# A recurrent attention layer with a soft mixture of experts: Gram quadrants, triangular blocks, transposed scans and outputs share banks, and the order is laid down anew

## The chip, the cores and the metric

One core of a Trainium2 chip runs the whole program. The time is device microseconds of one execution; several runs are taken and the median is given.

## The reference, cut to what matters

Inputs have batch 4, 8 heads, 768 positions and a head width of 40. The attention is a recurrence over positions, with a 40x40 state per batch and head:

```python
for t in range(S):
    y[:, :, t] = einsum('bhd,bhde->bhe', rt, state)
    Sa = einsum('bhde,bhe->bhd', state, at)
    state = state * wt[:, :, None, :] - einsum('bhd,bhe->bhde', Sa, bt)
    state = state + einsum('bhd,bhe->bhde', vt, kt)
```

Its output, 3072 rows of 320, goes through a soft mixture of experts: logits against 32 slots; a softmax over rows that gathers rows into slots; two matrix products (320 to 1024, a rectifier, 1024 to 320) for each of 8 experts; and a softmax over slots that spreads the result back. All of it is float32.

## The kernel before, in words

The 768 positions are cut into 12 stages of 64. The eight heads are taken in three groups `u` of 3, 3 and 2 heads (120, 120 and 80 partitions), for each of the 4 batches. In a stage:

- `scan_s`, `scan_k`, `scan_c` make running products of the decay `w` on DVE and multiply `k`, `b` and `a` by them ("wide products" of 120x768, on POOL or DVE).
- `lgram` makes the 32x32 triangular blocks of the products of `a` with `b`, and `gram` the other products of `a` with `k` and `b`: a part of 96 rows per batch (`qls`), and a quadrant of 32 rows per batch (`q0s`). Each result is cut by a mask as DVE takes it out of its PSUM bank.
- every second stage, `solve_in`, `solve_step` (30 of them, each a product and a sum, on DVE or POOL) and `solve_out` invert the triangular blocks. The very first solve is done in halves (`solve_half`, 14 steps), and `solve_join` puts the halves together by 256 small matmuls of 32x32x16: 64 in bank `jy` and, behind a copy, 64 in bank `jz`, and this for the first and the second stage of the pair.
- `chain_g`, `chain_u` (twice) and `chain_s` carry the state from stage to stage.
- `ctok_of` and `kbtok` transpose what the scans made; `y_vut`, `y_sd`, `y_p` and `y_y` make the stage's output, which goes into `xs` with the running product as a factor; the `slots_` functions feed the mixture of experts with every two stages.

Behind the last stage come the experts' products and 24 products that write the output.

All of this is recorded first as a list of operations with their dependences; eight PSUM banks are handed out as they come free. `forward` then lays the operations down, engine by engine, by a priority: the longest way to the end by its own table of costs, plus a shift per operation out of the string `SHIFT`. The string `SIDE` says for each operation that can run on two engines which of them takes it. The program's order on every engine is fixed by this. Where the planner expects TensorE to stand idle it puts in matmuls on constants (line 620, `filler`), whose results nobody reads. `HAM` and `FETCH` are its numbers for TensorE's clock and for the loading of instructions, `PACE` limits the bytes of loads in flight. Nearly every instruction carries line 1385 in the profile, that of the call that plans and emits; so the operands tell which is which: `wt` are the large work buffers, `ps` the banks, `cs_t` the constants, `mid` the buffer that holds the join's operands.

## Time and profile before

| | |
|---|---|
| median of 3 runs | 393.93 us |
| the three runs | 393.93, 388.39, 394.5 us |
| the profiled execution | 390.42 us |
| its span, first to last instruction | 388.3 us |
| TensorE: busy, share of the span | 347.5 us, 89% |
| VectorE (DVE): busy, share | 309.0 us, 80% |
| GpSimd (POOL): busy, share | 179.1 us, 46% |
| ScalarE (ACT): busy, share | 148.3 us, 38% |
| mean granted TensorE clock | 0.970 of full speed |

The profiled execution is 2.1 us longer than its span, for what lies before the first and behind the last instruction. PE is TensorE, PEld its loading of weights, SP the engine that issues the transfers. A busy PE is not PE at its peak, since matmuls overlap each other.

### The profile page before, as it was taken

The numbers are of one execution on the slowest core, as the hardware profiler recorded it, in microseconds if no ns is written. First come the engines' busy times: TensorE is split into PE (matmuls) and PEld (weight loads), VectorE is DVE, ScalarE is ACT, GpSimd is POOL, SyncE is SP. The second block draws the span as 40 slices with busy tenths as digits, with TensorE's granted clock in tenths as the row PEclk, the third lists the DMA queues.
The fourth block names the chain that finished last, engine by engine and source line by source line (L and its number), as shares of the span: only waits on it lengthen the run. The fifth ranks groups of instructions, "written<-read, shape, count | busy, mean of one in ns | idle before, by whom it ended". The sixth has DMA issues, their size and how long they took to land.

```text
span 388.3 us, 18515 instructions
## 1 busy us (share of the span) xinstructions
PE 347.5 (89%) x8179; PEld 301.5 (78%) x8179; DVE 309.0 (80%) x681; ACT 148.3 (38%) x311; POOL 179.1 (46%) x245
## 2 busy tenths in 40 slices
...
GB/s 280 382 205 285 2 45 45 126 100 71 89 163 125 68 147 112 165 102 41 137 137 122 184 111 117 104 254 183 184 128 213 282 202 197 255 329 149 2 101 307
DMA packets 37798, 60.66 MB, mean 156 GB/s; under 512 B 4695, under 2 KB 26967, under 8 KB 37719
## 3 DMA queue, kind: packets, MB, share of 16 engines
...
q8 instruction: 64, 1.05, 1.1%
...
## 4 chain that ended last, share of the span: by engine, by line
PE 57%; DVE 18%; issue 8%; DMA 7%; POOL 5%; ACT 3%; SPq 1%; DVEq 0%; POOLq 0%; ACTq 0%
PE ps L1385 56%; DVE wt L1385 11%; DMA wt<-in_kb_dram 5%; POOL wt L1385 4%; ACT wt L1385 2%; DVE mem L1385 2%; DVE ps L1385 2%; DMA wt<-in_aa_dram 1%; DVE old L1385 1%; SPq L1385 1%; DVE mid L1385 1%; PE ps L620 1%; POOL old L1385 1%; DMA wt<-in_rr_dram 0%; ACT mem L1385 0%
## 5 line engine op out<-in xcount | busy, mean ns | idle before, releaser
L1385 PE MATMUL ps<-wt,wt 128*64 128x40 f32 (+11 forms) x3576 | 163.8, 238 | 11.5 <-issue 7.2
L1385 PEld LDWEIGHTS ps<-wt,wt 80*32 80x32 f32 (+9 forms) x3576 | 142.8, 129 | 24.4 <-issue 11.2
L1385 POOL TENSOR_TENSOR old<-wt 128x130 f32<-128x130 f32 (+13 forms) x104 | 63.3, 608 | 61.1 <-DVE wt L1385 43.0
L1385 PE MATMUL ps<-cs_t,wt 120*128 120x120 f32 (+5 forms) x496 | 64.5, 267 | 12.2 <-ACT wt L1385 11.6
L1385 DVE TENSOR_TENSOR wt<-ps,cs_t 128x384 f32<-128x384 f32 (+6 forms) x132 | 61.6, 495 | 8.2 <-PE ps L1385 7.5
L1385 POOL TENSOR_TENSOR wt<-wt,wt 120x768 f32<-120x768 f32 x31 | 54.1, 1762 | 22.2 <-DVE wt L1385 14.4
L1385 POOL TENSOR_TENSOR wt<-wt,old 128x30 f32<-128x30 f32 (+13 forms) x92 | 51.6, 561 | 25.8 <-DVE old L1385 17.3
L1385 PEld LDWEIGHTS ps<-cs_t,wt 120*128 120x128 f32 (+5 forms) x496 | 50.5, 137 | 16.7 <-ACT wt L1385 12.2
L1385 ACT COPY wt<-ps 128x320 f32<-128x320 f32 (+3 forms) x62 | 30.0, 493 | 76.0 <-PE ps L1385 68.4
L1385 DVE TENSOR_TENSOR_SCAN wt<-wt,wt 120x780 f32<-120x780 f32 x24 | 44.1, 1838 | 1.7 <-DMA wt<-in_ww_dram 1.6
L1385 ACT COPY mem<-ps 120x480 f32<-120x480 f32 (+7 forms) x64 | 25.3, 412 | 35.5 <-PE ps L1385 31.6
L1385 ACT ACTIVATE wt<-ps 32x320 f32<-32x320 f32 x63 | 27.0, 429 | 30.4 <-PE ps L1385 19.0
L1385 PE MATMUL ps<-wt,mem 128*32 128x160 f32 (+4 forms) x448 | 36.9, 300 | 0.0
L1385 ACT ACTIVATE wt<-wt,bm_t 120x768 f32<-120x768 f32 (+1 forms) x36 | 28.6, 856 | 11.8 <-PE ps L1385 6.6
L1385 PE MATMUL ps<-mem 32*32 32x40 f32 (+2 forms) x776 | 32.4, 225 | 0.5 <-DVE wt L1385 0.4
L1385 PEld LDWEIGHTS ps<-wt,mem 128*32 128x32 f32 (+4 forms) x448 | 31.0, 137 | 1.7 <-issue 0.8
L1385 DVE COPY wt<-ps 128x320 f32<-128x320 f32 (+3 forms) x40 | 21.0, 544 | 7.0 <-PE ps L1385 6.7
L1385 ACT COPY wt<-wt 120x768 f32<-120x768 f32 (+3 forms) x19 | 16.2, 856 | 26.8 <-DVE wt L1385 26.7
L1385 DVE STREAM_TRANSPOSE wt<-wt 128x1024 f32<-128x1024 f32 x12 | 25.0, 2126 | 0.3
L1385 POOL MEMSET mem<- 128x2048 f32 x1 | 1.8, 1807 | 50.3 <-DVE mem L1385 50.3
L1385 DVE TENSOR_TENSOR wt<-wt,old 128x108 f32<-128x108 f32 (+16 forms) x65 | 23.3, 358 | 2.0 <-POOL old L1385 0.6
L1385 PEld LDWEIGHTS ps<-mem 32*32 32x32 f32 (+2 forms) x776 | 18.8, 116 | 7.5 <-issue 4.1
...
## 6 DMA issues: line engine op xcount, KB each, us to landing
...
```

Source lines behind the costliest of these rows:

```text
L620: self.nc.tensor.matmul(bank, lhs, rhs, start=True, stop=True)
L1385: nc.vector.memset(one_f, 0.0)
```

## The change

It makes these edits, beside new tables `SHIFT` and `SIDE` and some new numbers in the planner's model:

- `gram`: the quadrants of the three groups no longer stand beside each group's other products in its bank. They are made together, once the third group comes up, in a bank of their own, and one DVE instruction of 128x256 takes them out in place of three of 128x96, 128x96 and 128x64.
- `lgram`: the 24 products of a stage are recorded in one go at the third group rather than group by group.
- `ctok_of`: the first two groups share a bank and one copy of 128x480, in place of two of 128x240.
- `y_y`: likewise, the outputs of the first two groups share a bank, and one DVE product of 128x480 takes them out.
- `y_p`: the four products of a group, into two banks, are recorded as one operation.
- the planner's estimate of instruction loading, of TensorE's clock and of the loads in flight is changed, and the order comes out anew on each engine.

The program issues the same matmuls in the same shapes as before, 4,347 of them that compute, and 66 on constants where there were 65. Of DVE instructions there are 674 rather than 683, of ACT 298 rather than 313, of POOL 226 rather than 250; the transfers are the same in number and size. The solves' steps and sums stand 152 times on DVE (132 before) and 176 times on POOL (196 before), the wide products 10 times on DVE (6) and 28 times on POOL (32).

```diff
--- before.py
+++ after.py
@@ -126,50 +126,49 @@
 TURN = dict(PE=-70, DVE=32, ACT=18, POOL=0)
 
 
-FETCH = (256, 146, 447, 1150, 2350, 0.45)
+FETCH = (256, 146, 447, 1300, 2350, 0.5, 500)
 FILL = (900, 500, 225)
-HAM = (3413, 0.135, 1.8, 110, 0.165)
+HAM = (3413, 0.145, 1.8, 110, 0.18)
 HEAT = (0.15, 60e3, 470, 385, 400)
 DMA = (720, 1350, 1500, 1.05)
 
 CLASH = dict(DVE=138, POOL=190)
 
 ISSUE = 420
-PACE = (500e3, 60e3, 256e3, 1400e3)
+PACE = (500e3, 60e3, 256e3, 1000e3)
 WIDE, SLIM = 0.632, 1.15
 WAIT = 1500
 START = ((225, 210), (195, 195))
 ROUNDS = 0
 STEP = {**{chr(79 + v): v for v in range(-44, 46)}, "~": 13, "!": -45}
 SHIFT = (
...
 )
 SIDE = (
...
 )
 LOOK = dict(PE=1, DVE=130, ACT=1, POOL=130, SP=1)
 
@@ -632,7 +631,7 @@
                 x += m * step
                 if (self.seen - FETCH[1]) % FETCH[0] == 0:
                     r = max(x, self.there[-1] if self.there else 0.0)
-                    self.there.append(r + FETCH[3] + FETCH[5] * max(0.0, dma - r) + FETCH[4])
+                    self.there.append(r + FETCH[3] + FETCH[5] * max(0.0, dma - r - FETCH[6]) + FETCH[4])
                 if (self.seen - FETCH[2]) % FETCH[0] == 0:
                     i = (self.seen - FETCH[2]) // FETCH[0]
                     if 0 <= i < len(self.there) and self.there[i] > x:
@@ -969,15 +968,22 @@
             nc.copy_a.copy(kbks[st].rearrange("p (b c) -> p b c", b=B)[:, :, H0[u] * D:H0[u] * D + n],
                            tp[:, 0:4 * n].rearrange("p (b c) -> p b c", b=B))
 
+        ctl = {}
+
         def ctok_of(st, u):
             if u == 0:
                 ctoks.put(st)
             n = NHU[u] * D
-            tp = bank(f"tp_cs{st}")
+            if u != 1:
+                ctl[st] = bank(f"tp_cs{st}")
+            tp = ctl[st]
+            m, a = (2 * 3 * D, 3 * D * u) if u < 2 else (n, 0)
             for i in range(2):
                 o = (B * u + 2 * i) * C
-                nc.tensor.transpose(tp[:, i * n:(i + 1) * n], cps[st][0:n, o:o + 128], ident[0:n, 0:n])
-            nc.copy_a.copy(ctoks[st][:, :, H0[u] * D:H0[u] * D + n], tp[:, 0:2 * n].rearrange("p (i c) -> p i c", i=2))
+                nc.tensor.transpose(tp[:, i * m + a:i * m + a + n], cps[st][0:n, o:o + 128], ident[0:n, 0:n])
+            if u:
+                c = slice(0, m) if u == 1 else slice(H0[u] * D, H0[u] * D + n)
+                nc.copy_a.copy(ctoks[st][:, :, c], tp[:, 0:2 * m].rearrange("p (i c) -> p i c", i=2))
 
         def gram(st, u):
             if u == 0:
@@ -993,30 +999,34 @@
                 o = slice(b * w, (b + 1) * w)
 
                 nc.tensor.matmul(gr[0:96, o], k_t.rearrange("p q k t -> p (q k t)")[:, 0:96], bd[0:n, 0:nh, b, 32:64], start=True, stop=True)
-            for b in range(B):
-
-                nc.tensor.matmul(gr[32 * b:32 * b + 32, 4 * w:5 * w], kbt(st)[0:n, B * u + b, 0, 0], bd[0:n, 0:nh, b, 0:32], start=True, stop=True)
             nc.vector.tensor_tensor(
                 qls[st][0:96, 12 * u:12 * u + 4 * nh], gr[0:96, 0:4 * w].rearrange("p (h t) -> p h t", t=32),
                 mask_q[0:96].unsqueeze(1).broadcast_to([96, 4 * nh, 32]), ALU.mult)
-            nc.vector.tensor_tensor(
-                q0s[st][:, H0[u]:H0[u] + nh], gr[:, 4 * w:5 * w].rearrange("p (h t) -> p h t", t=32),
-                mask_s.unsqueeze(1).broadcast_to([128, nh, 32]), ALU.mult)
+            if u == NU - 1:
+                gq = bank(f"gq{st}")
+                for v in range(NU):
+                    n, o = NHU[v] * D, 32 * H0[v]
+                    for b in range(B):
+                        nc.tensor.matmul(gq[32 * b:32 * b + 32, o:o + 32 * NHU[v]], kbt(st)[0:n, B * v + b, 0, 0],
+                                         bds["a", st][0:n, 0:NHU[v], B * v + b, 0:32], start=True, stop=True)
+                nc.vector.tensor_tensor(q0s[st], gq[:, 0:256].rearrange("p (h t) -> p h t", t=32),
+                                        mask_s.unsqueeze(1).broadcast_to([128, H, 32]), ALU.mult)
 
         lps = {}
 
         def lgram(st, u):
-            nh = NHU[u]
-            n = nh * D
-            bd = bds["a", st][:, :, B * u:B * u + B]
-            if u == 0:
+            if u == NU - 1:
                 lps[st] = bank(f"ls{st}")
-            lp = lps[st].rearrange("p (q h t) -> p q h t", q=2, t=32)
-            for q in range(2):
-                for b in range(B):
-                    nc.tensor.matmul(lp[32 * b:32 * b + 32, q, H0[u]:H0[u] + nh], (bbs[st][0:n, B * u + b, q] if st < 2 else kbt(st)[0:n, B * u + b, q, 1]),
-                                     bd[0:n, 0:nh, b, 32 * q:32 * q + 32], start=True, stop=True)
-            if u == NU - 1:
+                lp = lps[st].rearrange("p (q h t) -> p q h t", q=2, t=32)
+                for v in range(NU):
+                    nh = NHU[v]
+                    n = nh * D
+                    bd = bds["a", st][:, :, B * v:B * v + B]
+                    for q in range(2):
+                        for b in range(B):
+                            x = bbs[st][0:n, B * v + b, q] if st < 2 else kbt(st)[0:n, B * v + b, q, 1]
+                            nc.tensor.matmul(lp[32 * b:32 * b + 32, q, H0[v]:H0[v] + nh], x,
+                                             bd[0:n, 0:nh, b, 32 * q:32 * q + 32], start=True, stop=True)
                 ss, p = st // 2, st % 2
                 if p == 0:
                     lls.put(ss)
@@ -1175,6 +1185,8 @@
                 nc.tensor.transpose(tp[0:n, b * n:(b + 1) * n], sold[0:n, grp(u, b)], ident[0:n, 0:n])
             nc.copy_a.copy(sd[0:n, 0:4 * n], tp[0:n, 0:4 * n])
 
+        yyl = {}
+
         def y_p(st, u):
             nh = NHU[u]
             n = nh * D
@@ -1182,12 +1194,14 @@
             vut = vuts[NU * st + u]
             bd = bds["r", st][:, :, B * u:B * u + B]
             pp = ppb.put(NU * st + u)
-
-            for i in range(2):
-                g = bank(f"ppp{st}")
+            gs = [bank(f"ppp{st}") for _ in range(2)]
+            nc.gather = True
+            for i, g in enumerate(gs):
                 for x in range(2):
                     nc.tensor.matmul(g[:, 2 * w * x:2 * w * (x + 1)], vut[0:n, 2 * i + x], bd[0:n, 0:nh, 2 * i + x],
                                      start=True, stop=True)
+            nc.gather = False
+            for i, g in enumerate(gs):
                 nc.vector.tensor_tensor(pp[:, 2 * i:2 * i + 2, 0:nh], g[:, 0:4 * w].rearrange("p (i h t) -> p i h t", i=2, t=64),
                                         mask_p.unsqueeze(1).unsqueeze(1).broadcast_to([128, 2, nh, 64]), ALU.mult)
 
@@ -1198,21 +1212,25 @@
             n = nh * D
             sold = st_of.get(st)
             pp = ppb[NU * st + u]
-            yp = bank(f"yps{st}")
+            if u != 1:
+                yyl[st] = bank(f"yps{st}")
+            yp = yyl[st]
+            m, a = (2 * 3 * D, 3 * D * u) if u < 2 else (n, 0)
             for i in range(2):
                 bx = [(b, slice(64 * (b % 2), 64 * (b % 2) + 64)) for b in (2 * i, 2 * i + 1)]
+                o = i * m + a
                 if sold is not None:
                     for b, r in bx:
-                        nc.tensor.matmul(yp[r, i * n:(i + 1) * n], rts[st][0:n, B * u + b],
+                        nc.tensor.matmul(yp[r, o:o + n], rts[st][0:n, B * u + b],
                                          sds[NU * st + u][0:n, b * n:(b + 1) * n], start=True, stop=False)
                 for j in range(nh):
                     for b, r in bx:
-                        o = i * n + j * D
-                        nc.tensor.matmul(yp[r, o:o + D], pp[:, b, j], kbks[st][:, head(b, H0[u] + j)],
+                        nc.tensor.matmul(yp[r, o + j * D:o + j * D + D], pp[:, b, j], kbks[st][:, head(b, H0[u] + j)],
                                          start=(sold is None), stop=(sold is None or j == nh - 1))
-            c = slice(H0[u] * D, H0[u] * D + n)
-            nc.vector.tensor_tensor(xs[st][:, :, c], yp[:, 0:2 * n].rearrange("p (i c) -> p i c", i=2),
-                                    ctoks[st][:, :, c], ALU.mult)
+            if u:
+                c = slice(0, m) if u == 1 else slice(H0[u] * D, H0[u] * D + n)
+                nc.vector.tensor_tensor(xs[st][:, :, c], yp[:, 0:2 * m].rearrange("p (i c) -> p i c", i=2),
+                                        ctoks[st][:, :, c], ALU.mult)
 
         def xtile(i, j):
             return xs[2 * i + j // 2][:, j % 2]
```

What the new tables do to the order is seen at two places. The first is PE around the first solve's join. In the rows before, `mid,wt_72` of 32x16 are the products into `jy`, `wt_74,mid` of 32x16 those into `jz`, and `cs_t` alone marks matmuls on constants:

```order
L620 MATMUL ps_67<-cs_t 128x128 x9
L1385 MATMUL ps_67<-wt_77,wt_70 32x96 x8
L1385 MATMUL ps_67<-wt_77,wt_70 32x64 x8
L1385 MATMUL ps_67<-wt_77,wt_70 32x96 x8
L1385 MATMUL ps_63<-mid,wt_72 32x16 x64
L1385 MATMUL ps_62<-mid,wt_72 32x16 x64
L1385 MATMUL ps_67<-wt_74,mid 32x16 x64
L1385 MATMUL ps_63<-wt_77,wt_70 32x64 x4
L620 MATMUL ps_62<-cs_t 128x448
```

In the changed kernel:

```order
L619 MATMUL ps_61<-cs_t 128x128 x6
L1403 MATMUL ps_66<-mid,wt_72 32x16 x64
L1403 MATMUL ps_66<-wt_77,wt_70 32x96 x16
L1403 MATMUL ps_66<-wt_77,wt_70 32x64 x8
L1403 MATMUL ps_63<-wt_77,wt_70 32x96 x8
L1403 MATMUL ps_63<-wt_77,wt_70 32x64 x4
L1403 MATMUL ps_68<-wt_77,wt_70 96x96 x4
L1403 MATMUL ps_66<-wt_77,wt_70 96x64 x4
L619 MATMUL ps_62<-cs_t 128x128 x10
L1403 MATMUL ps_61<-wt_74,mid 32x16 x64
L1403 MATMUL ps_61<-wt_77,wt_70 96x96 x4
L1403 MATMUL ps_63<-wt_74 32x40 x2
```

Where 192 products of the join stood in a row, 64 now stand at a time, and a stage's triangular blocks (32x96 and 32x64 out of `wt_77,wt_70`), Gram products (96x96, 96x64) and 10 matmuls on constants stand between them; the second half of the join comes later, behind the first products of `chain_u` (`wt_74`, 32x40).

The second place is DVE ahead of the join, where the two transposes `wt_74<-wt_72` and `mid<-wt_72` hand the halves to it. Before:

```order
L1385 TENSOR_TENSOR wt_72<-wt_72 128x2x14
L1385 STREAM_TRANSPOSE wt_74<-wt_72 128x32x32
L1385 SCALAR_TENSOR_TENSOR wt_71<-wt_70,wt_71 120x780
L1385 STREAM_TRANSPOSE mid<-wt_72 128x16x32
L1385 TENSOR_TENSOR mem<-ps_61,cs_t 128x96
L1385 TENSOR_TENSOR mem<-ps_68,cs_t 128x96
L1385 TENSOR_TENSOR wt_72<-ps_67,cs_t 128x512
L1385 STREAM_TRANSPOSE wt_72<-wt_72 128x32x32
L1385 TENSOR_TENSOR wt_77<-wt_70,wt_71 120x12
L1385 RECIPROCAL wt_71<-wt_77 120x12
L1385 SCALAR_TENSOR_TENSOR wt_70<-wt_70,wt_71 120x780
L1385 COPY mid<-ps_62 128x16x16
```

In the changed kernel:

```order
L1403 TENSOR_TENSOR wt_72<-wt_72 128x2x14
L1403 STREAM_TRANSPOSE wt_74<-wt_72 128x32x32
L1403 STREAM_TRANSPOSE mid<-wt_72 128x16x32
L1403 SCALAR_TENSOR_TENSOR wt_71<-wt_70,wt_71 120x780
L1403 TENSOR_TENSOR wt_77<-wt_70,wt_71 120x12
L1403 RECIPROCAL wt_71<-wt_77 120x12
L1403 TENSOR_TENSOR mem<-ps_68,cs_t 128x256
L1403 TENSOR_TENSOR wt_72<-ps_66,cs_t 128x512
L1403 STREAM_TRANSPOSE wt_72<-wt_72 128x32x32
L1403 SCALAR_TENSOR_TENSOR wt_70<-wt_70,wt_71 120x780
L1403 TENSOR_TENSOR wt_77<-wt_77,bm_t 120x36
```

The scan (`SCALAR_TENSOR_TENSOR` of 120x780) that stood between the two transposes now stands behind both, and a single 128x256 takes out a stage's quadrants where rows of 128x96 stood.

## Rows read from the trace of the kernel before

**Rows 1.** The page: busy time and its share of the span, by engine; instructions.

```profile
PE 347.5 (89%) x8179; PEld 301.5 (78%) x8179; DVE 309.0 (80%) x681; ACT 148.3 (38%) x311; POOL 179.1 (46%) x245
PE 57%; DVE 18%; issue 8%; DMA 7%; POOL 5%; ACT 3%; SPq 1%; DVEq 0%; POOLq 0%; ACTq 0%
```

**Rows 2.** Busy time by stretch, in the columns that its first line names.

```profile
core 0: us, PE busy (x) PEld busy (x) DVE busy (x) ACT busy (x) POOL busy (x), PEclk, DMA share, GB/s
0.00:50.00 50.00, 36.48 (x548) 33.98 (x548) 42.78 (x76) 20.68 (x36) 24.43 (x18) 1.00 0.73 232
50.00:66.00 16.00, 11.04 (x513) 8.39 (x514) 15.71 (x28) 5.99 (x10) 11.29 (x13) 0.68 0.10 30
66.00:100.00 34.00, 31.04 (x993) 27.70 (x992) 23.72 (x51) 8.33 (x16) 26.27 (x37) 1.00 0.33 95
100.00:260.00 160.00, 154.48 (x3769) 137.54 (x3769) 147.86 (x316) 74.38 (x148) 101.20 (x149) 0.99 0.44 128
260.00:350.00 90.00, 85.43 (x1961) 74.11 (x1960) 70.97 (x189) 29.32 (x74) 15.91 (x29) 0.98 0.70 218
```

**Rows 3.** PE's first work and around the join: start us, us, what, [idle before, its end].

```profile
9.24 1.33 PE L1385 MATMUL ps<-cs_t,wt 80*128 80x80 f32 x6 [9.24 <-ACT wt L1385]
...
52.55 1.29 PE L1385 MATMUL ps<-mid,wt 32*32 32x16 f32 x133 [1.27 <-DVE mid L1385]
54.17 1.55 PE L1385 MATMUL ps<-mid,wt 32*32 32x16 f32 x122 [0.32 <-issue]
57.50 1.89 PE L1385 MATMUL ps<-wt,mid 32*32 32x16 f32 x124 [1.70 <-issue]
61.23 0.43 PE L1385 MATMUL ps<-wt,wt 80*32 80x64 f32 x4 [1.48 <-issue]
```

**Rows 4.** DVE in the same form, ahead of the join.

```profile
47.79 2.13 DVE L1385 STREAM_TRANSPOSE wt<-wt 128x1024 f32<-128x1024 f32 x1
49.82 1.73 DVE L1385 TENSOR_TENSOR_SCAN wt<-wt,wt 120x780 f32<-120x780 f32 x1
51.48 1.02 DVE L1385 STREAM_TRANSPOSE mid<-wt 128x512 f32<-128x512 f32 x1
```

**Rows 5.** Busy time in three of the stretches of 2 us around the join.

```profile
54.00:56.00 2.00, 1.63 (x127) 1.52 (x128) 1.93 (x4) 0.69 (x2) 1.06 (x1) 0.66 0.03 8
56.00:58.00 2.00, 0.50 (x37) 0.50 (x40) 2.00 (x4) 0.98 (x2) 1.11 (x2) 0.50 0.00 0
64.00:66.00 2.00, 2.00 (x48) 1.51 (x40) 1.89 (x3) 1.23 (x3) 1.84 (x3) 0.78 0.00 0
```

**Rows 6.** DVE by shape: busy us, mean ns of one, then idle before and what ended it.

```profile
L1385 DVE TENSOR_TENSOR mem<-ps,cs_t 128x96 f32<-128x96 f32 x16 | 3.7, 245 | 0.0
L1385 DVE TENSOR_TENSOR wt<-ps,cs_t 128x256 f32<-128x256 f32 x24 | 9.5, 416 | 1.4 <-PE ps L1385 1.2
L1385 DVE TENSOR_TENSOR mid<-ps,mem 128x240 f32<-128x240 f32 x12 | 4.7, 402 | 2.9 <-PE ps L1385 2.7
L1385 DVE COPY wt<-ps 128x480 f32<-128x480 f32 x6 | 3.9, 652 | 0.1
L1385 DVE TENSOR_SCALAR wt<-ps 32x320 f32<-32x320 f32 x33 | 16.1, 488 | 9.7 <-PE ps L1385 5.3 <-ACT wt L1385 3.8
```

**Rows 7.** The solve's steps and the wide products, on DVE and on POOL.

```profile
L1385 DVE TENSOR_TENSOR wt<-wt,old 128x108 f32<-128x108 f32 (+16 forms) x65 | 23.3, 358 | 2.0 <-POOL old L1385 0.6
L1385 DVE TENSOR_TENSOR wt<-wt,wt 120x768 f32<-120x768 f32 x6 | 6.3, 1060 | 1.1 <-issue 1.1
L1385 POOL TENSOR_TENSOR old<-wt 128x130 f32<-128x130 f32 (+13 forms) x104 | 63.3, 608 | 61.1 <-DVE wt L1385 43.0 <-ACT wt L1385 12.7
L1385 POOL TENSOR_TENSOR wt<-wt,wt 120x768 f32<-120x768 f32 x31 | 54.1, 1762 | 22.2 <-DVE wt L1385 14.4 <-DMA wt<-in_kb_dram 3.0 <-DMA wt<-in_b_dram 2.4
```

**Rows 8.** DVE and POOL side by side, by the timeline.

```profile
45.85 1.90 DVE L1385 TENSOR_TENSOR wt<-wt 128x28 f32<-128x28 f32 x2
46.02 1.68 POOL L1385 TENSOR_TENSOR wt<-wt,wt 120x768 f32<-120x768 f32 x1 [8.64 <-DVE wt L1385]
```

More of the change, by code (lines that the diff above doesn't have):

```diff
@@ L160 @@
[L160 to L163 removed]
+    r"zOG1MYE(J;;WS_%Z~EOfIc!Iee-!c,Ob#SoUX@NPD?9OlNHPOOT4KOa/]bdbNK~%O!N6Q+E8OBM6OAOO27rIXl4O!#CF[^3OOEQ44JQODQHN%SIF"
@@ new lines @@
+    r"jTf[5OP#[VMIOA5#FCDX7LO6W_NH!Mj!P2KL?OO!O={&+:OOWO`KV2Q^]QOH~`HGX!b&4lonGR_fGCL:NLUAMN7K$~N(O5HKCN-j[M~vkf;|;Ocl"
+    r"D?xOP^wsZW!(^@g*M!!3HjNSJYh5A,FB~DH@cKHON~:=nbK`@]((gK_PBK8IwjNSC;ON'/%'BUpCCFSb<$n5F7!CSNGV9MGXSUKtx_ELecaVv5<'"
+    r"rOO^MbW{7ZFCW,;T.]P&FtR|n2P-|CS0UP;T#x)5Udg!TRZ<SqO8|<Jsl4i`Q7OO[Mag!FQm*m~$O6[KO3uSSO!QNGOO61^#M`aw|OO#d1YN~7pE"
+    r"iQa|`wZLd~~gv|x|%;CHOZORRxqC|RA-UR_2KARxONMu]gIOODCPM~;UO4S9|H@kai6OTKbO{uSGO!{9HnSOf-XCM1SR?Qcq|_H]|O=HUOOfYdA!"
+    r"`3i4IBf*p!Fg@_04?=NU<d*G=>71_KWtVWZdmBksstwn;lZMojTF`'$/xdRAD[g6I~>~!1@UCM!C2!;O%!O]/qOOOI!J?E<7-O73!?L|1P>k.'UO"
@@ new lines @@
+    r"G34S|_Xq|Yd?aZcw{_u>|2yvoyZc|_Mae5Ng]WU_#O%<Q>$R-OZbSgH>HwO3NkNVoLZOj]sONCROcz{mTVOfMsGD+1p)GxSE0M?$_|#4'X?*s!~L"
+    r"jO0#/|3_TOKOQ|OcYT|gk^^nFn'p|zfOscT|||jT|]r|=['^3NP?WCOE[O/O|PZP2Tc];R(c?O?R!S9MhOO;QC;wtq!OE1iRRMEvUmw`cH]g<OUZ"
+    r"9!8$B@M~I&C2]gcW>DsH!A@NNU|FPKkZ9E@XAN13mtO2BN8QAKa-YNrK{qe{RD7W='=mSCQ'TImVYYdZH|;GHO[N>zn{|qRqJ5;t-8KG:1;E-_68"
+    r"i.;!XRHxN0OK4IU%W!BLTOplFIQ!TT$|zKEJ{KOO]:OC`hqzgMDJON]S]RJ8xUJhYYF@hO3)LdU-Q~#2o@LUP>Lf3*BA<6lg[XZ-YUjLl_RS&9=S"
+    r"Oz:H/O1VN.OihM<OiV^VjVTOjFdcL!2iJwTOl,ZkUN)I^AOOHJ=wB0I]b|J|YLUu3_ZSJPnj*]OPXRP:OOM3=8RZHTb-OdhEZ;DC!QeFOH;!5POO"
@@ new lines @@
+    r"GRs07U,^p!6Hg.|MOVzw^/mNe|Furq;W|R]xjrEPOOOVRaq?RO|RDNSXVFQ@+g/=4g8QW[|hfN6!>KGE_fqM[ajJ!U*@L>e<S[HDWG,U`lONPIUJ"
+    r"[gZOJK/?FOAT.DhT8OGI;7||YHnD1BDT15JN!bsvp^Q^LcORFR]`<T>XOeO*L_bqfwiUUUOZ=fy:O5m/;O9Qa.]zOOdH`'OMh9ej<W,*4OE@I*_G"
+    r"JGTLT/OY*eODYVeO%S|/yR{j[8T=JPO~O5VR?I.Hd!!@-!sD8!6R!<'>>O!MqI,H!QL(CCJQKO@zQL9O`%GY>b!g<9FY!_vN>S-E$)QzPWMDNQFa"
+    r"Q^R|8WRcmOOZ4?NBN=IOCOwOy~rtdMV2@|]O|3c{`R_YMzk^qRe{wrW4p7SUOu=Ju#]=|HmXEmO|OO2COW||ZOxY8fZuZ>RPOiQI`OONo4[HKbJs"
+    r"lSO5MjlT?<LVM=UMj;O[>U~fR/xJ4R!3rOCDY!:qDER-**QyWH.:JQO!?>~&OR=EIM[F`,Qt`MM>Oz9bYQ&k/4|MzJOONIROuGG'[KDOTi{kUP&<"
@@ L164 @@
+    r"R8O;._v!LtGF:P^FXV!c~kOSOjOSWY{pv|JFBOp7|YOO?A@XG^3CTA!!CU*>6/+43,r#Lw!+:FbDL^DNL<UTGF@!0FBMQ!B&OO|(UiO|<O)]XYUU"
+    r"Ytk|1W|HkOt[q[|OWJX@;9-M1R2Y+?k6O8BK0O*A:5W7N274B^Ngc_&h='"
 )
 SIDE = (
-    r"0101001011001100110010000011000011100100000011001000000101101011110101110110110010111111111111111111101111101001"
-    r"0011011111111111111110000101111100111111010101101111101111111101101111111011110111111111111111111111110101110000"
-    r"1111000101011111101001111100100010011111001111111100101110100111111101001101110111101111101111101111111110111111"
@@ L169 @@
-    r"1100011001100000011111111101111001001000101001111111011110101110011111111111111110111011111011011001111111111111"
-    r"1111110010010001000111110110000111110001100010001110111000001000101101111001011111110111110110110110010011110110"
-    r"0010011110011010011011010010110101000011101101111011011000011001011101000110111101110000000011101101100100111000"
-    r"00111111100010111100011101001000110010111"
+    r"0001000110111001001111000100000110000000011000000000110101010101111111100000001111001001101010011001010111011111"
@@ new lines @@
+    r"1010100100101000010110111110111100010111110011111111111111010100110111110011111110111111111000010111111001011010"
+    r"0100111001110001001100111111111111001101111011111111010111100001010011100110000111111100111111101111110111111011"
+    r"1110001111010101011010011010111110101111011111110011111011111001111111111100101110110100111110010110111101110010"
+    r"0011101010100101111100110101011000011111101101101110010001101100011101111111010010110111011010000111011000010101"
+    r"1101101010110111100100100000000010001010101000101110010001001011101110100110111111111111110100011000111010010001"
@@ L173 @@
+    r"11011000100100001110001101101"
 )
```

19 lines of the change are left out of this document (removed).

## The prediction

> **What bounds the kernel now.** I read the page first: PE is busy for 89% of the span, DVE for 80%, and of the chain that ended last 57% is PE and 18% DVE [rows 1]. An average over stages says little, so the table by stretch comes next [rows 2]. From 100 to 350 us PE stands idle for 160 - 154.48 and 90 - 85.43, together 10.1 of 250 us: there it sets the pace. DVE has 160 - 147.86 = 12.1 us free between 100 and 260 us, so it is close behind. The slack is in the opening. In the first 50 us PE works for 36.5, part of it on constants, and its first matmul waits for ACT until 9.24 us [rows 3]; DVE is busy for 42.8 of them. From 50 to 66 us PE works 11.0 of 16 us at a mean granted clock of 0.68 [rows 2]. The two levels are 2.4 GHz and, at a reading of 0.50 [rows 5], 1.2 GHz, so 16 x (1 - 0.68) / 0.5 = 10.2 us ran at the lower one. Before and as it fell, PE did nothing but the join's 32x32 products.
>
> The profiled execution took 390.42 us, 3.5 below the median of 393.93; the three runs lie between 388.39 and 394.5. The sum is made against 390.4. Two per cent, about what a measurement of this kernel can tell from no change, is 7.9 us of the median: faster means below 386.05, slower above 401.8.
>
> **What does not change.** The matmuls are the same in number and shape. The time that PE computes comes back whole; a gain must come from idle time, the low clock or waits. So the merged banks as such bring PE nothing. What covers them is that PE goes on with other groups while an eviction runs; if all eight banks were held it would wait for the longer eviction, 0.65 in place of 0.40 us, 0.25 us each time [rows 6].
>
> **The opening: the step that I count on.** Three terms.
>
> (a) The transpose that hands the join its second operand stood behind a scan: 47.79 for the first transpose, then 1.73 us of scan, then the one of 1.02 us, and PE waited for it for 1.27 us, beside filling matmuls [rows 3, 4]. The scan now stands behind both. The join can start 1.73 us earlier; behind it stand now, as before, a product and a reciprocal of 120x12 for a later stage, which nobody on the join's way reads. I take -1.7. The bounds are 0 (something else late) and -1.7.
>
> (b) The join's products ran into stalls that end at nothing the profile shows, 1.70 and 1.48 us [rows 3]. The first followed 133 + 122 matmul records of this kind, the second another 124. In the changed order 64 products stand at a time, with Gram products of 96x96 between. The instructions are as many, but they are used up more slowly, so loading them has more time. I take half, -1.6; bounds 0 and -3.2, and +3.2 if such stalls come elsewhere.
>
> (c) The clock. At the full clock 133 records took 1.29 us, 9.7 ns each; at the lower one 124 took 1.89 us, 15.2 ns each, 1.57 times as long [rows 3]. Of the 10.2 us, 3.2 are those stalls and 7.0 are work, which at the full clock would take 7.0 / 1.57 = 4.5: the low clock costs 2.5 us. With larger products between the quadrants the clock should hold longer, but `chain_u` and the second half of the join still follow, so I take half, -1.3; bounds 0 and -2.5. The Trainium skill, TensorE: Matmul & The Clock Gate, section HAM oscillation, puts the penalty at the throttled time times one less the clock ratio, which here would be 10.2 x 0.5 = 5.1 us; the sum would be 1.3 lower by it, at half. The row on the quadrants speaks for less.
>
> Together -4.6, between -7.4 and +3.2.
>
> On SP the constants move from fourth to sixth place, behind a further 128x768 and 128x512 of float32, 655 KB; at the 232 GB/s of that stretch [rows 2] they land 2.8 us later. PE's first transposes need them, but those wait for ACT until 9.24 us [rows 3] and DVE, not PE, is the busier engine up to 50 us. Nothing, then; without that cover at most 2.8 us.
>
> **The middle: DVE gives and takes.** Gram quadrants: 36 instructions, each at most 0.245 us, become 12 of 0.416 [rows 6]. Of the 36, 24 are of 96 and 12 of 64; at an estimated 0.21 for those of 64, 8.4 becomes 5.0, -3.4. Outputs: 24 of 0.402 become 12 of 480 columns, priced by the copy of 128x480 at 0.652: 9.6 to 7.8, -1.8. The copies of the scans save likewise, mostly on ACT (38% busy), where it costs and brings nothing. Against that, 20 solve steps move from POOL to DVE at 0.358: +7.2; four wide products at 1.060: +4.2; four evictions of 32x320 at 0.488 from ACT: +2.0 [rows 6, 7]. DVE ends up with 8 us more, POOL with 20 x 0.6 + 4 x 1.762 = 19 less. The 8 us fit into the 12.1 free between 100 and 260 us, so I count them at nothing; PE is the cover, and where it stands ready early they are on the path, up to +8. The shorter steps (0.358 for 0.608, 20 times, 5 us over the solves) count at nothing too: a solve is wanted only two stages later.
>
> A new order can also take away some of PE's 10.1 us of idle time or add to it. Nothing in the trace of before shows which; I take 0, with bounds of -5 (half of it gone) and +8 (all of DVE's work on the path).
>
> **The tail.** The large weights' loads move in SP's queue; with fewer bytes allowed in flight a load of 640 KB could come one load later, 640 KB / 218 GB/s = 2.9 us [rows 2]. From 260 to 350 us PE was busy for 85.4 of 90, which says that loads were not what held it. 0, at worst +2.9.
>
> Sum: 390.4 - 4.6 = 385.8 us.
>
> **Rivals.**
>
> DVE becomes the bound. Place: the solves between 100 and 260 us. The moved steps read two SBUF operands, and POOL works beside them: at 45.85 us two such steps of 128x28 took 1.90 us together, against 0.358 for one as a mean over larger ones, while a wide product ran on POOL for 1.68 [rows 7, 8]. If one step in four of the 20 and the four wide products pay 1.2 us more, that is 9 x 1.2 = 11 on top of 8: 19 less the 12.1 us free adds 7 us, and where DVE's free time cannot be used (a third of it, between operands that are not ready) 11. It decides from 12 us of additional work on. Without the opening's gain, 390.4 + 11 = 401; with all of the free time lost, 409. Against it: POOL has 19 us less to do. Chance 0.11. The Trainium skill, SBUF — State Buffer, section on SBUF's two sides, has DVE and GpSimd lock their shared ports for a whole instruction, so that one blocks: by that rule, moving work onto DVE while POOL is busy buys less than its price. The trace agrees, with the 1.90 us.
>
> The opening gives nothing. PE's work is unchanged; what the join gains is lost again at the next wait, since from 66 to 100 us PE was idle for another 3.0 us and POOL busy for 26 of 34 [rows 2]. Then 390 us. For it: PE's busy share behind 100 us leaves nothing to catch up. This is also the case where the change does not do what it says: sparing evictions that nobody waited for. Chance 0.28.
>
> The new order helps everywhere: the opening near its bound of -7.4 and 5 of the 10.1 us idle behind 100 us gone, 378 us. For it: those idle times are many short ones, some at stalls like those of the join. Against: nothing named in the change is aimed at them. Chance 0.18.
>
> **How the numbers follow.** The forecast has 0.43, with 382 to 389 as its own range; it sits on the border, so half of it counts as faster. Faster: 0.22 and nearly all of the 0.18, with 0.02 of the second rival's spread, 0.42. Slower: half of the first rival and a little of the rest's spread, 0.07. Same: 0.51. A range that leaves out a fifth: from 377, under the third rival, to 396, which takes in the opening's gain cancelled by 8 us of DVE and the run-to-run 394.5, and leaves out most of the first rival.
>
> **What would show it.** Each step has its place in the changed profile. (a) The join's first 32x16 products start about 2 us before 52.5. (b) No stall above 1 us between them. (c) Less than 10 us at the low clock up to 70 us. Middle: PE idle from 100 to 350 us still about 10 us, DVE's busy time 317 rather than 309, the 128x256 and 128x480 instructions at 0.42 and 0.65 us. The prediction fails if DVE's idle time in the middle is used up and PE waits for it, if the first join starts no earlier, or if the low clock turns up in a new place of the middle.

## The result, and the profile after

The changed kernel takes 386.62 us in the median of 20 runs (384.44 to 394.88), the kernel before, beside it, 391.75 us in the median of 20 (388.39 to 395.46). The ratio is 0.9872, with a 95% interval from 0.9841 to 0.9902: a gain of 1.3%, under the two per cent that count as faster. The forecast was 385.8 us. The ratios here and below leave out the runs that took over 1.5% longer than the fastest of their kernel; medians, means and the fit below are of all runs. The runs of one kernel lie 7 to 10 us apart, mostly with the clock that they were granted; so what is shown here is an execution of 386.07 us (span 384.3 us, clock 0.970), to stand beside the one of 390.42 us (span 388.3 us, clock 0.970) before. The first profile of the changed kernel fell in an execution of 392.36 us (clock 0.945); it is called the first profile below.

The page first, the lines that answer to [rows 1], for the changed kernel:

```profile
PE 345.3 (90%) x8181; PEld 303.6 (79%) x8181; DVE 314.4 (82%) x672; ACT 146.0 (38%) x296; POOL 163.9 (43%) x221
...
PE 59%; DVE 18%; issue 8%; POOL 7%; DMA 3%; ACT 3%; DVEq 0%; POOLq 0%; ACTq 0%
```

The span is 4.0 us shorter. PE's busy time fell by 2.2 us, from 347.5, and its idle time by 1.8, from 40.8 to 39.0. DVE has 5.4 us more work, POOL 15.2 less. The same table by stretch as [rows 2], of the changed kernel, says where:

```profile
core 0: us, PE busy (x) PEld busy (x) DVE busy (x) ACT busy (x) POOL busy (x), PEclk, DMA share, GB/s
0.00:50.00 50.00, 34.68 (x524) 32.19 (x524) 43.82 (x73) 19.21 (x30) 24.29 (x18) 0.97 0.71 231
50.00:66.00 16.00, 13.57 (x554) 12.92 (x557) 12.16 (x22) 4.62 (x9) 6.21 (x8) 0.79 0.24 69
66.00:100.00 34.00, 31.50 (x906) 27.23 (x894) 31.82 (x67) 13.79 (x26) 17.18 (x21) 0.95 0.26 75
100.00:260.00 160.00, 154.69 (x3960) 140.11 (x3956) 148.50 (x303) 70.08 (x134) 101.57 (x151) 0.99 0.43 124
260.00:350.00 90.00, 85.47 (x1913) 72.35 (x1914) 69.88 (x186) 29.54 (x75) 14.63 (x25) 1.00 0.72 222
```

In the first 50 us PE stands idle for 1.8 us longer (15.3 for 13.5) and is busy for that much less. From 100 to 350 us PE stands idle for 5.31 + 4.53 = 9.8 us (10.1 before): little changed there. From 50 to 100 us it stands idle for 2.43 + 2.50 = 4.9 us, where it was 4.96 + 2.96 = 7.9 [rows 2]: 3.0 us less. But the clock up to 100 us is worse: by the column PEclk, (50 x 0.03 + 16 x 0.21 + 34 x 0.05) / 0.5 = 13.1 us at the lower level, against 10.2. Around the join there is less of it, 6.7 us from 50 to 66 us; the rest lies in two stretches in which the order of before has the full clock, at 33 to 37 us and at 71 to 74 us. Over the whole span the two executions have the same clock, 0.970.

PE around the join, in the form of [rows 3]; a product of the join or on constants stands as two records, so x128 are 64 of the former and x20 ten of the latter:

```profile
9.54 1.30 PE L1403 MATMUL ps<-cs_t,wt 80*128 80x80 f32 x6 [9.54 <-DMA cs_t<-in_consts_dram]
...
50.94 1.25 PE L1403 MATMUL ps<-mid,wt 32*32 32x16 f32 x128 [1.93 <-DVE mid L1403]
52.67 4.62 PE L1403 MATMUL ps<-wt,wt 120*32 120x96 f32 x88 [0.48 <-ACT mid L1403]
57.09 4.11 PE L619 MATMUL ps<-cs_t 128*128 128x128 f32 x20
61.12 1.26 PE L1403 MATMUL ps<-wt,mid 32*32 32x16 f32 x128
62.92 0.92 PE L1403 MATMUL ps<-wt,wt 120*96 120x96 f32 x8 [0.53 <-DVE wt L1403]
...
65.22 1.05 PE L1403 MATMUL ps<-mid,wt 32*32 32x16 f32 x103 [0.48 <-issue]
...
69.61 1.50 PE L1403 MATMUL ps<-wt,wt 96*32 96x40 f32 x50 [2.04 <-issue]
```

The join starts at 50.94 us, 1.6 earlier. The stalls without a named cause between its products, 1.70 and 1.48 us before, are down to one of 0.48; one of 2.04 stands at 69.61, behind the join's third lot. And the constants are now what PE's first matmul waits for, 0.3 us later than before. DVE ahead of the join shows why it starts earlier (compare [rows 4]):

```profile
47.81 2.09 DVE L1403 STREAM_TRANSPOSE wt<-wt 128x1024 f32<-128x1024 f32 x1
49.81 0.99 DVE L1403 STREAM_TRANSPOSE mid<-wt 128x512 f32<-128x512 f32 x1
50.67 1.71 DVE L1403 TENSOR_TENSOR_SCAN wt<-wt,wt 120x780 f32<-120x780 f32 x1
```

The merged evictions and the moved products on DVE, by shape, to set beside [rows 6, 7]; the last row is POOL's:

```profile
L1403 DVE TENSOR_TENSOR mid<-ps,mem 128x480 f32<-128x480 f32 x6 | 3.9, 649 | 2.5 <-PE ps L1403 2.5
L1403 DVE TENSOR_TENSOR mem<-ps,cs_t 128x256 f32<-128x256 f32 x8 | 3.2, 398 | 0.0
L1403 DVE TENSOR_TENSOR wt<-wt,wt 120x768 f32<-120x768 f32 x10 | 9.4, 951 | 0.1
...
L1403 POOL TENSOR_TENSOR wt<-wt,wt 120x768 f32<-120x768 f32 x27 | 48.6, 1812 | 28.3 <-DVE wt L1403 20.2 <-DMA wt<-in_kb_dram 5.5 <-DMA wt<-in_b_dram 2.6
```

One costs 0.65, 0.40 and 0.95 us, where 0.65, 0.42 and 1.06 were taken; the wide products on DVE are no slower beside a busy POOL. It is POOL that can be held up: its sum of 128x30 takes 0.27 us at 103.26 us, but beside a DVE instruction that reads two work buffers it ends only as that one ends, in 1.41 us at 58.41 (to 59.82, the wide product to 59.72), in 1.59 at 109.45 (to 111.04, a scan to 111.01) and in 1.79 at 155.99 (to 157.78, a scan to 157.75).

### The profile page after: what moved, and what is told of

It reads as the page before. It is cut to its first block, busy times and chain, and to the rows that moved or that the text cites. A ratio compares the mean times of both kernels' runs of the same rounds, so it can differ in the third digit from the quotient of the medians.

```text
span 390.6 us, 18480 instructions
## 1 busy us (share of the span) xinstructions
PE 352.9 (90%) x8181; PEld 310.8 (80%) x8181; DVE 314.8 (81%) x672; ACT 146.1 (37%) x296; POOL 162.4 (42%) x221
## 4 chain that ended last, share of the span: by engine, by line
PE 64%; DVE 17%; issue 6%; DMA 4%; POOL 4%; ACT 2%; SPq 1%; DVEq 0%; ACTq 0%; POOLq 0%
PE ps L1403 61%; DVE wt L1403 12%; PE ps L619 4%; POOL wt L1403 2%; POOL old L1403 2%; DMA cs_t<-in_consts_dram 2%; DMA wt<-in_w_dram 1%; DVE old L1403 1%; DVE mem L1403 1%; DVE ps L1403 1%; DMA mem<-in_rr_dram 1%; ACT wt L1403 1%; SPq L1403 1%; DVE mid L1403 1%; ACT mem L1403 1%
## 5 line engine op out<-in xcount | busy, mean ns | idle before, releaser
L1403 PE MATMUL ps<-wt,wt 96*32 96x40 f32 (+10 forms) x3576 | 166.5, 243 | 6.2 <-issue 3.3
L1403 PEld LDWEIGHTS ps<-wt,wt 120*32 120x32 f32 (+8 forms) x3576 | 149.8, 133 | 16.6 <-issue 7.3
L1403 POOL TENSOR_TENSOR old<-wt 128x168 f32<-128x168 f32 (+15 forms) x96 | 53.7, 559 | 64.5 <-DVE wt L1403 46.4
L1403 DVE TENSOR_TENSOR wt<-ps,cs_t 128x384 f32<-128x384 f32 (+4 forms) x124 | 60.5, 514 | 7.9 <-PE ps L1403 7.3
L1403 POOL TENSOR_TENSOR wt<-wt,old 128x30 f32<-128x30 f32 (+14 forms) x79 | 51.0, 646 | 37.9 <-DVE old L1403 31.3
L1403 PEld LDWEIGHTS ps<-cs_t,wt 120*128 120x128 f32 (+5 forms) x496 | 51.5, 139 | 15.3 <-ACT wt L1403 10.8
L1403 POOL TENSOR_TENSOR wt<-wt,wt 120x768 f32<-120x768 f32 x27 | 47.4, 1766 | 29.6 <-DVE wt L1403 21.9
L1403 ACT ACTIVATE wt<-ps 32x320 f32<-32x320 f32 x59 | 25.3, 428 | 34.0 <-PE ps L1403 29.6
L1403 ACT COPY mem<-ps 120x480 f32<-120x480 f32 (+7 forms) x56 | 24.3, 452 | 30.4 <-PE ps L1403 26.1
L1403 DVE TENSOR_TENSOR wt<-wt,old 128x210 f32<-128x210 f32 (+16 forms) x78 | 27.1, 348 | 4.5 <-POOL old L1403 3.0
L1403 DVE TENSOR_SCALAR wt<-ps 32x320 f32<-32x320 f32 x37 | 18.0, 487 | 7.6 <-PE ps L1403 4.7
L1403 PEld LDWEIGHTS ps<-wt 32*32 32x32 f32 x1536 | 16.9, 108 | 8.3 <-issue 4.7
```

The lines of the kernel that those rows point to most:

```text
L1403: nc.vector.memset(one_f, 0.0)
```

## The experiments

The theory to test: **the gain is the order's**, above all the opening's, and the merged evictions are worth nothing by themselves. Its rival: the merges save time on an engine that PE waits for. The edits are given in short.

**1. The changed kernel once more.**

> The changed kernel, unaltered, for another profile: the first one fell in an execution of 392.4 us with three stretches of 10.2 us at the low clock, while its median is 386.6. Theory A (the gain is in the opening, in the join's order and its stalls and clock): a profile near 386 us has the join's products start up to 2 us before 52.5 us, stalls around it below 3 us, and less than 10 us at the low clock up to 80 us. Theory B (the gain is spread over the middle, where evictions are fewer): the opening up to 66 us is as long as before, and the same work behind it is done in some 5 us less.

385.62 us (median of 2), ratio 0.9822 [0.9714, 0.993]. This is the profile shown above.

**2 to 4. The kernels without their tables.** In all three `SHIFT` and `SIDE` are empty, so that the planner's own costs set the order.

```diff
-SHIFT = (...)
-SIDE = (...)
+SHIFT = ""
+SIDE = ""
```

The first is the kernel before; the second the changed code with the planner's old numbers; the third the changed code with its new numbers.

> The kernel before with its two tables of shifts and sides left empty, so that only the planner's own priorities set the order. It is the base for the next two; both theories expect it to be slower than the kernel before, an estimate is 3 to 8% (403 to 422 us), since more of the waits that the tables took away come back.

> The changed kernel with the merged banks, evictions and recordings, but without tables and with the planner's old numbers: against the plain kernel before, this is the merges alone. Theory A (PE sets the pace, the merges spare DVE work that nobody waits for): the same within 4 us. Theory B (the merges are the gain): 5 us faster or more.

> The same with the planner's new numbers: against the run before it, this is the numbers alone, without tables. Both theories expect the same within 4 us, since the numbers only steer an order that no table has tuned; a rival on loads (fewer bytes in flight bring the first weights of the experts late) expects up to 3 us slower, at 350 us and behind.

| without tables | median, us | ratio to the kernel before, with tables |
|---|---|---|
| code of before | 424.14 | 1.0675 [1.0526, 1.0823] |
| changed code, old numbers | 428.18 | 1.0908 [1.0823, 1.0993] |
| changed code, new numbers | 425.48 | 1.0829 [1.0737, 1.0921] |

The first came out above the 403 to 422 us that were estimated. The edits without a fitted order bring nothing, if anything a loss of up to 2%. The tables are worth 7 to 10%, more than five times the change. Whether the code of before, with tables fitted anew, would gain as much was not tried; that rival stays open.

**5. The merges undone within the changed order.** Each merged eviction is cut again, at its place, and the order of everything else stays.

```diff
-  nc.vector.tensor_tensor(q0s[st], gq[:, 0:256]..., mask_s..., ALU.mult)
+  # three, one per head group: 128x96, 128x96, 128x64
+  nc.vector.tensor_tensor(q0s[st][:, H0[v]:H0[v] + NHU[v]], gq[:, 32 * H0[v]:...]..., mask_s..., ALU.mult)
   # the products of the outputs and the copies of the scans: 128x480 into 2 x 128x240
```

> The changed kernel in its own order, but with the evictions cut again as before: each quadrants' product of 128x256 into three (128x96, 128x96, 128x64), each outputs' product and each scans' copy of 128x480 into two of 128x240. DVE gets some 5 us more of work (24 instructions more at the quadrants, 12 at the outputs), ACT some 2. Theory A (the middle has room on DVE, the merges are worth nothing by themselves, the gain is the order's): no more than 1 us slower than the changed kernel, DVE busy about 319 us instead of 314. Theory B (the gain of the middle is the DVE time that the merges save): 3 to 5 us slower, so all the gain is gone.

386.19 us (median of 12), ratio 0.9884 [0.9845, 0.9922], the same as the changed kernel's 0.9872. DVE had its 5.4 us more and PE did not mind, by the page's busy times of this kernel, and by its stretch from 100 to 260 us:

```profile
PE 349.2 (90%) x8181; PEld 306.1 (79%) x8181; DVE 319.8 (82%) x713; ACT 146.5 (38%) x303; POOL 163.4 (42%) x221
```

```profile
100.00:260.00 160.00, 154.48 (x3852) 139.78 (x3849) 148.96 (x318) 70.50 (x138) 101.34 (x149) 0.98 0.42 122
```

Its PE busy time is higher because this execution's clock was 0.958. PE idles for 5.52 us in that stretch, with the merges for 5.31. Theory A holds, to within the 0.4% of the interval: what the merged evictions save lies under PE's work.

**6 and 9. The scan's place, taken back in the changed order, and changed in the order of before.** One DVE instruction moves, the rest of the order stays.

```diff
 # 6, the changed order
-DVE: transpose wt, transpose mid, scan
+DVE: transpose wt, scan, transpose mid
 # 9, the order of before
-DVE: transpose wt, scan, transpose mid
+DVE: transpose wt, transpose mid, scan
```

> The changed kernel in its own order, but on DVE the one scan of 1.7 us stands again between the two transposes ahead of the join. Theory A (the opening gave its 1.7 us back by 72 us, so the scan's place is worth nothing at the end): the join's first product at about 52.7 us instead of 50.9, the end within 0.5 us of the changed kernel. Theory B (what the join gains early lasts to the end, as the prediction had it): 1.7 us slower.

> The kernel before in its own order, but on DVE the one scan of 1.7 us that stands between the two transposes ahead of the join is put behind both of them. Theory A (the scan's place is worth its time in whatever order it stands): the join's first product at about 50.9 us instead of 52.6, the end 1 to 1.7 us earlier. Theory B (only the changed order can use the earlier start, here what follows waits for other things): the join as early, but the end within 0.5 us of the kernel before.

Number 6: 390.46 us (median of 12), ratio 1.0003 [0.9943, 1.0063]. Beside the changed kernel's runs that is 1.3% slower by the ratios, 3.8 us by the medians and 2.4 us by the means (389.9 for 387.5). Its profiled execution, though, took 386.02 us at a clock of 0.967, no longer than the one shown of the changed kernel (386.07 us at 0.970). Number 9: 390.31 us (median of 12) beside 391.83, ratio 0.9961 [0.9921, 1.0], 1.5 us faster with an interval that just reaches no change. The profiles show where the 1.7 us go, first PE around the join in number 6, then in number 9:

```profile
53.57 1.25 PE L1414 MATMUL ps<-mid,wt 32*32 32x16 f32 x128 [3.59 <-DVE mid L1414]
...
59.73 2.45 PE L630 MATMUL ps<-cs_t 128*128 128x128 f32 x20
62.42 1.26 PE L1414 MATMUL ps<-wt,mid 32*32 32x16 f32 x128 [0.23 <-DVE wt L1414]
```

```profile
51.46 1.29 PE L1396 MATMUL ps<-mid,wt 32*32 32x16 f32 x133
54.39 1.27 PE L1396 MATMUL ps<-mid,wt 32*32 32x16 f32 x123 [1.64 <-issue]
...
57.68 1.89 PE L1396 MATMUL ps<-wt,mid 32*32 32x16 f32 x124 [1.92 <-issue]
...
61.68 0.43 PE L1396 MATMUL ps<-wt,wt 80*32 80x64 f32 x4 [1.75 <-issue]
```

In the changed order the wait for DVE rises from 1.93 to 3.59 us, just the scan. In the order of before the wait of 1.27 us for DVE is gone, and the stalls without a named cause grow from 3.5 to 5.3 us in the same place (4.3 in number 10): what PE gained by an earlier operand it lost to them, and at the third lot it stood at 57.68 us, against 57.50 before. The trace shows what they wait for. Instructions come in by a queue of their own, 64 transfers of 16 KB in a run; two of these land at 52.74 and 56.20 us before and at 52.95 and 56.43 us in number 9, though the join starts 1.1 us earlier there, and PE goes on 1.2 to 1.5 us behind each. So by this trace the scan's place is worth nothing in the order of before, as Theory B has it; the runs of number 9 do not decide between the two theories.

How much of what number 6 lost is the scan? The clock tells part of it. Each run lists its mean granted clock c, so 2 x (1 - c) x span is its time at the lower level. Over the 130 runs of the kernel before, the changed one and numbers 5 to 9, a fit with one level for each kernel and one slope gives 0.39 us (0.06 either way) for each us at the lower clock. The slope is not the same for all: by itself the kernel before gives 0.51 (0.12 either way) and the changed one 0.35 (0.10), and over the 92 runs that the ratios use the common one is 0.28 (0.07). At 25 us of low clock the levels are:

| kernel | us at 25 us of low clock | mean low clock, us |
|---|---|---|
| before | 391.2 +- 0.5 | 26.1 |
| changed | 386.1 +- 0.7 | 28.8 |
| 5, merges undone | 385.6 +- 1.0 | 28.9 |
| 6, scan taken back | 386.9 +- 1.0 | 32.7 |
| 7, ten products on constants less | 386.1 +- 1.2 | 38.0 |
| 8, eight products on constants earlier | 385.3 +- 1.4 | 34.1 |
| 9, before with the scan moved | 390.7 +- 0.9 | 24.5 |

At equal clock the change is worth 5.1 +- 0.9 us (4.7 +- 0.9 over the 92 runs). Its 2.7 us more of low clock are not clear of the spread: 28.8 +- 2.8 for 26.1 +- 0.9, with medians of 26.2 and 26.3. The scan alone is worth 0.8 +- 1.2; of the 2.4 us that number 6 lost by the means, the fit puts the other 1.5 to its 3.9 us more of low clock. Whether the scan's place sets the clock, or 12 runs met it by chance, stays open.

**7 and 8. The products on constants.** From 57.09 to 61.12 us the changed kernel runs ten such products ahead of the join's third lot, at the low clock. Number 7 leaves them out; number 8 puts eight of them behind the join's first lot instead, two ahead of each of four operations.

```diff
 # 7
+del self.extra[op of the join's third lot]
 # 8
+for q in (lgram 3, gram 3 quadrants, gram 3 u=0, gram 3 u=1):
+    self.extra[q] = (2, ...)
```

> The changed kernel in its own order without the ten products on constants ahead of the join's third lot of products; on the chip they take 4.1 us there, from 57.1 to 61.2 us, at the low clock. Theory A (these products, at half the clock, hold the join up by more than the wait that they were to fill, and that is where the opening's gain went): the third lot starts 1.5 to 2.5 us earlier and the end comes 1 to 2 us earlier. Theory B (the join waits there for DVE or ACT anyway, or the clock stays low for longer without them): no gain, or up to 2 us slower, with more low clock behind 61 us.

> The changed kernel in its own order; the ten products on constants ahead of the join's third lot are taken out, and eight such products stand behind the join's first products instead, two ahead of each of four operations from 52.2 to 56 us, in which the granted clock is still full. Theory A (the clock falls at 54 us because of the narrow products before, wider ones among them hold it up): no low clock from 54 to 61 us, and the end 1 to 3 us earlier. Theory B (the clock falls all the same, and the eight products only cost their 0.25 us each): low clock from 54 us on as in the changed kernel, the end 0 to 2 us later than without any of them.

Number 7: 391.47 us (median of 12), ratio 0.9966 [0.9925, 1.0007]; number 8: 388.56 (median of 6), 0.9886 [0.983, 0.9943]. Theory B has the sign of number 7, but not its size: by the medians it is 4.9 us slower than the changed kernel, where up to 2 were given. Number 8 is 1.9 us slower than the changed kernel and 2.9 faster than number 7, where Theory B gave 0 to 2 slower than without any. PE in number 7, then in number 8:

```profile
52.31 1.25 PE L1405 MATMUL ps<-mid,wt 32*32 32x16 f32 x128 [0.44 <-DVE mid L1405]
...
56.42 1.15 PE L1405 MATMUL ps<-wt,wt 120*96 120x96 f32 x11 [0.25 <-issue]
60.30 1.90 PE L1405 MATMUL ps<-wt,mid 32*32 32x16 f32 x128 [2.73 <-DVE wt L1405]
```

```profile
53.28 1.22 PE L624 MATMUL ps<-cs_t 128*128 128x128 f32 x4 [0.46 <-ACT mid L1408]
54.43 1.94 PE L1408 MATMUL ps<-wt,wt 120*32 120x96 f32 x48
56.30 1.22 PE L624 MATMUL ps<-cs_t 128*128 128x128 f32 x4
57.45 1.08 PE L1408 MATMUL ps<-wt,wt 120*32 120x96 f32 x24
```

Without the ten, the third lot follows the first by 8.0 us rather than 10.2, and Theory A is right so far; but PE waits for DVE for 2.73 us in that place, and the clock stays low for longer: 38.0 us in the mean of the runs, where the changed kernel has 28.8. With eight early ones the clock fell all the same: it is 0.61 from 52 to 54 us and 0.50 from there to 62 us. The filling products hold the third lot up by 2 us and are still worth their place, for the clock's sake: by the fit, the 9.2 us more of low clock in number 7 make 3.6 us, nearly all that it lost by the means (391.2 for 387.5).

**10. The kernel before, profiled again.** No edit.

> The kernel before as it is, for a second profile of it. Theory A (the time in which TensorE waits for nothing that the profile shows belongs to the order): again 11 to 12 us of it, in about 13 places, the same places as in the first profile, against 7.7 to 8.6 us in four of the five profiles of the changed order. Theory B (it varies from one execution to the next): 8 to 9 us here too, and then 3.5 us of the gain are not to be put down to it.

391.82 us. PE's largest waits, in total, with their number and the longest, for this second profile of before, then for the changed kernel:

```profile
PE ps L1385 <- issue: 12.6, 14, 2.5
PE ps L1385 <- ACT wt L1385: 12.6, 6, 9.0
PE ps L1385 <- DVE mem L1385: 2.0, 3, 1.1
PE ps L1385 <- DVE wt L1385: 1.9, 5, 0.6
PE ps L1385 <- DVE mid L1385: 1.3, 1, 1.3
```

```profile
PE ps L1403 <- DMA cs_t<-in_consts_dram: 9.5, 1, 9.5
PE ps L1403 <- issue: 8.0, 11, 2.0
PE ps L1403 <- DVE wt L1403: 3.9, 8, 0.9
PE ps L1403 <- DVE mem L1403: 2.8, 3, 1.8
PE ps L1403 <- DVE mid L1403: 1.9, 1, 1.9
...
PE ps L1403 <- ACT wt L1403: 1.0, 1, 1.0
```

Theory A holds: the order of before has 11.5, 12.4 and 12.6 us of stalls without a named cause in its three profiles (numbers 9 and 10 among them), the changed order 8.0, 7.7, 7.7, 8.6 and 5.5 in those of numbers 1, 5, 7, 8 and 6, and 8.3 in the first profile. Most come back at the same products: x124 of the join at 57.50 and 58.60 us before, x50 of 96x40 at 69.61 us in number 1 and 70.97 us in number 6. By these two profiles 4.6 us are gained there, and 2.1 more where PE waited for ACT or, at the start, for the constants; waits for DVE (8.6 us for 5.2) give 3.4 back.

The times of the instruction queue's transfers, which the traces hold packet by packet, say what these stalls are. The page of the kernel before has this line for that queue (packets, MB, share); the other profiles of these two orders have 64 transfers as well:

```profile
q8 instruction: 64, 1.05, 1.1%
```

The nine profiles have 91 such stalls, 82 us in all. Of these, 89 end 1.2 to 1.7 us behind the landing of such a transfer (1.4 in the median), where a moment taken at random does so one time in ten; the other two lie ahead of the first landing. So they are waits for instructions to be loaded.

**11 and 12. One table without the other.** The changed code with `SIDE` alone (11) and with `SHIFT` alone (12).

```diff
 # 11
-SHIFT = (...)
+SHIFT = ""
 # 12
-SIDE = (...)
+SIDE = ""
```

> The changed kernel's code and numbers with its table of engines alone: no shifts of priority. Theory A (most of what the tables bring is which engine takes an operation, with DVE taking over slow steps from POOL): 395 to 405 us, DVE busy over 305 us, POOL under 170. Theory B (it is mainly the shifts, the order within the engines): 413 to 425 us, near the 425 without tables.

> The changed kernel's code and numbers with its table of shifts alone: every operation that may run on two engines takes the engine that it names first. Theory A (the engines carry the tables' gain): 415 to 428 us. Theory B (the shifts carry it): 390 to 405 us. If neither alone comes below 415, the two tables only work together, as one order.

413.42 us, ratio 1.0528 [1.0432, 1.0624], with the engines alone; 422.25, 1.0774 [1.0698, 1.0851], with the shifts alone. From the 425.48 without tables that is 12 and 3 us; both together bring 39. With the engines alone DVE is busy for 325.9 us and POOL for 164.0, as Theory A had it, but the time stays at the edge of what Theory B gave; and with the shifts alone it is no better. So 24 of the 39 us come only when engines and order fit each other. No kernel here beats the changed one by more than the runs can tell.

## Why the prediction was right, point by point

The total was right, 385.8 for 386.6, and in part by luck: two errors cancel. From the profiled 390.42 us, at which the sum starts, 4.6 us were to go; the execution shown is 4.35 us shorter, 1.8 of them PE's idle time, 2.2 its busy time and the rest outside the span. Up to 100 us PE's idle time fell by 1.2 us only (1.8 more, then 3.0 less), so the gain is not the opening's alone.

(a) The scan: right at its place. From the start of the first transpose to the end of the second DVE takes 2.99 us instead of 4.71, and number 6 takes that back. In the executions shown the join's first product starts at 50.94 instead of 52.55 us, 1.6 for the 1.73 taken; other executions have it elsewhere (52.85 us in the first profile, 53.17 in number 10). To the end the scan carries less, 0.8 +- 1.2 us at equal clock, which may be nothing.

(b) The stalls around the join: right in kind, mis-sized. Half of 3.2 us was taken; from 50 to 66 us they fell from 3.5 us to 0.48, the whole of it. That they are waits for instructions was argued there and is borne out by the landings above: around the join, four transfers land 3.5 to 4.0 us apart before (52.74, 56.20, 59.78, 63.81 us), and in the changed kernel three lie between 53.72 and 63.76 us. The 2.04 us at 69.61 are no new cost: such stalls took 2.5 us from 66 to 100 us both before and after. Together (a) and (b) were to bring 3.3 us, and PE's idle time from 50 to 100 us fell by 3.0.

(c) The clock: this step failed. Of the 10.2 us at the lower level half was to go, for -1.3 us. Around the join 3.5 us did go (6.7 us are left from 50 to 66 us), but 3.0 us ahead of it and 3.4 behind it are new, 13.1 us up to 100 us in all; the sign that was given, less than 10 us up to 70 us, holds by a hair, with 9.7. The place at the join is not safe either: the first profile has 10.2 us there, and so has number 8, which put more large products in. Over all runs the low clock is the same within the spread, so the term brought nothing that can be told. The step's price was near: a factor of 1.57 means 1 - 1/1.57 = 0.36 us for each us, and the common fit gives 0.39 +- 0.06. The Trainium skill, TensorE: Matmul & The Clock Gate, section HAM oscillation, would make it 0.5; the kernel before by itself agrees with that (0.51 +- 0.12), the changed one speaks for less (0.35 +- 0.10). The factor goes with the shape: from number 1 at the full clock to number 7 at 0.50, the 32x16 products of the third lot went from 1.26 to 1.90 us (1.51 times), x64 of 32x40 from 0.79 to 1.29 (1.63), x8 of 120x96 from 0.92 to 1.60 (1.74) and x2 of 128x448 from 1.02 to 1.86 (1.82).

The constants on SP were taken as nothing, with 2.8 us at most; they cost 0.3, 9.54 us for 9.24, with the DMA now as what ends last.

"The time that PE computes comes back whole": this failed too, the other way, and it hid the miss of (c). In the three profiles of the order before PE is busy for 347.5, 349.5 and 348.5 us at clocks of 0.970, 0.966 and 0.970; in those of numbers 1, 6 and 5 for 345.3, 345.6 and 349.2 at 0.970, 0.967 and 0.958. With 0.36 us taken off for each us at the lower clock that is 339.1, 340.0 and 340.1 before, and 337.0, 336.5 and 337.5 after (337.4 in the first profile): 2.7 us less for the same products. By shape the triangles' and quadrants' products and those of `y_p` stand out, all of which are now made in one go. Before, then changed:

```profile
L1385 PE MATMUL ps<-wt,mem 120*128 120x192 f32 x96 | 20.0, 339 | 0.0
L1385 PE MATMUL ps<-wt,wt 120*32 120x96 f32 x544 | 18.1, 249 | 1.3 <-ACT wt L1385 0.5 <-DVE wt L1385 0.3
L1385 PE MATMUL ps<-wt,wt 80*32 80x64 f32 x272 | 9.6, 226 | 3.6 <-issue 2.7 <-ACT wt L1385 0.6 <-POOL wt L1385 0.2
```

```profile
L1403 PE MATMUL ps<-wt,mem 120*128 120x192 f32 x96 | 18.0, 330 | 0.1
L1403 PE MATMUL ps<-wt,wt 120*32 120x96 f32 x544 | 17.0, 259 | 1.5 <-issue 0.6 <-ACT mid L1403 0.5 <-POOL wt L1403 0.4
L1403 PE MATMUL ps<-wt,wt 80*32 80x64 f32 x272 | 8.5, 227 | 0.0
```

The mean of one changed little, yet the group is busy for less: matmuls in a row overlap each other, and fewer groups begin and end alone. Part of a group's loss is only how overlapping ends of two groups are counted; PE's whole busy time counts each moment once. The products of `y_p` (120x192 and 80x128), summed by shape, take 53 to 54 us in all profiles of the code of before, number 2 among them, and 49 to 50 in all of the changed code with its new numbers, number 4 among them (number 3, with the old numbers, has 51.5); so the code makes most of that difference, with tables or without. That it is the cause of the 2.7 us was not tried by itself, and numbers 2 to 4 show that it brings nothing to the time in an order that is not fitted: the cause stays open.

The middle: right. PE idles there for 9.8 us rather than 10.1, and DVE's additional work (5.4 us, priced at 8) is covered. Number 5 adds the evictions' 5.4 us again and finds cover for them too, so the first rival, DVE as the bound, was far off (its 1.2 us more for each blocked instruction is what the trace had for two together): DVE's busy time from 100 to 260 us rose by 0.6 us only, since part of its work moved to the stretch from 66 to 100 us, where it went from 23.7 to 31.8 us. The tail: right, PE's idle time behind 350 us is 8.9 us for 9.3.
